# A transformer block on one core: block 0's divisions beside the projections, output projections ahead of the preceding block's last sums, and a tail that is written out

## The chip, the cores and the metric

The kernel runs on one core of a Trainium2 chip. A core has five engines with a queue of instructions each: TensorE (PE; its weight loads are listed apart as PEld), VectorE (DVE), ScalarE (ACT), GpSimd (POOL) and SyncE (SP), which issues nearly all DMAs here. The metric is device time in microseconds. The kernel before takes 1800.45 us, the median of 3 runs (1799.79 to 1802.5).

## The reference

One transformer block with adaptive layer norm, on 2048 rows of width 512, all in float32:

```python
mod = (_silu(c) @ w_mod).reshape(c.shape[0], 6, 1, -1)
sa, ca, ga, sb, cb, gb = (mod[:, i] for i in range(6))
h = _layernorm(x) * (1 + ca) + sa
x = x + ga * attention(h, wqkv, wo)          # 32 heads of 16, softmax over all 2048 keys
h = _layernorm(x) * (1 + cb) + sb
x = x + gb * (gelu_tanh(h @ w1 + b1) @ w2 + b2)   # 512 -> 1792 -> 512
```

The inputs are drawn large (the weights of the attention times 8, those of the feed-forward part times 64), so the softmax needs its row maxima.

## The kernel before, in words

**Precision.** Operands of TensorE are split into a high part (rounded to fp32r) and a low part (the remainder). A product is three matmuls: high by high, low by high, high by low. A "group" is the list of such terms that add into one bank of the matmul accumulator.

**Rows.** The 2048 rows are 4 blocks of 512 (`NB`, `TB`). A block's way after attention is: four *divisions* (`o_prep(b, k)`, one for each quarter of the 512 columns, that is for 8 heads); the output projection with residual (4 groups of 12 terms, one for each 128 rows); layer norm; 4 transposes with modulation; 14 pieces of the first feed-forward layer (`ffn1(i)`, 12 terms each) with the Gelu; and the sums of the second layer, in three parts (`PARTS`), 4 groups each. The last of these parts here is called the block's last sums.

**The attention loop.** There are 32 units: 4 blocks of queries by 8 sets of 4 heads. Each unit has 16 half steps of 128 keys, 512 in all (`half_step`). A half step issues 4 score matmuls (`e`, L623), whose exponent ScalarE takes (`p`, L628), 4 matmuls for the row maxima (`mx`, L382), whose maximum VectorE takes (`mxp`, L387), and the sums over values (`pv`, L652, 4 matmuls with 8 records). The maxima need a whole pass over the keys before the unit's first exponent, so they run `LEAD` = 84 matmuls ahead of the scores; a unit has 64. When a unit's 64 are done, VectorE and GpSimd make a high and a low part of the maxima, SP stores them to DRAM (`m<-m`, L408) and loads them back as two extra rows of the scaled queries (`qst<-m`, L414). The unit's first `e` waits for that load.

**Background work.** Beside the loop, one bank (number 7, named `bg`) takes the groups of projections and feed-forward work: six matmuls of half the rows each (`RUN` = 6) in a half step, the upper and lower 64 rows in turn. A generator hands out the groups in a written order (`work`): first `block0` (the query, key and value projections that are still missing, then `open_ffn`, which closes old buffers and opens new ones), then `ffn_block(0)`, `(1)`, `(2)`. It hands out nothing while its condition isn't met, and then the half step has no background work: the last score matmul of the step sits in bank 7 instead.

**The clock.** Work on other engines is put into the program by a count: `advance` adds 1 to it with each exponent, so 4 in a half step, and `later(n, f)` issues f after n counts. In the engines' queues everything then stands in the order in which it was issued. The division of `o_prep` is such a chain: SP loads the sums of exponents (`dn<-ou`, L682) and the sums over values (`ob`); 14 counts on VectorE inverts them (L692); SP stores them to DRAM (`rden`, L696) and loads them back spread over the heads' rows (`rb<-rden`, L700); then one engine multiplies and splits (L704 to L706): GpSimd, but VectorE for block 3. At most two divisions are under way, and none starts before `open_ffn` has run.

```python
        eng = gp if b < NB - 1 else ve
...
        later(14, inv)
...
        if not ready or "f" not in pools:
            return
```

**Weights.** `wload` (L738) issues on SP the loads of the split weights, in the order of a list (`stream`), into 8 buffers in turn, one in each second half step; a load waits on SP until the buffer's last matmul is done. Behind the loop 6 more buffers come.

**The Gelu.** In the loop it is taken apart: ScalarE takes a tanh, and GpSimd does seven instructions for each piece (L853 to L863). Only block 3, behind the loop, uses ScalarE's own Gelu (`evac_tail`).

**Behind the loop** (L1040 on, the tail) the matmuls have all 128 rows and 7 banks in turn. What is left of block 2 is handed out in turn with block 3's projection and norm: the generator of block 3 (`last`) is asked first, and where it has nothing, block 2's groups come. The last unit's sums still have to go through their division there.

Of the kernel before, what the change touches and what calls it, by code (L numbers as in the profile page):

```python
# [16 lines left out]
P = 128  # L17
S = 2048
D = 512
# [18 lines left out]
LEAD = 84  # L38
# [24 lines left out]
PARTS = ((0, 6), (6, 12), (12, NF))  # L63
AHEAD = 2
# [5 lines left out]
def block_kernel(ctx: ExitStack, tc: tile.TileContext, x, wqkv, wo, w1, b1, w2, b2, c, w_mod, out):  # L70
# [71 lines left out]

    hcm, hpool = pool("hT", side="right")
    hT = [[hpool.tile([P, KC, TB], FR, name=f"hThi{b}"), None] for b in range(NB)]
# [24 lines left out]
    def load_x(b, q=sy):  # L169

        xin[b] = hpool.tile([P, 4, D], F32, tag=f"lo{b}", name=f"xin{b}", bufs=1)
# [296 lines left out]
    def low_x(b, f, e):  # L468
        if hT[b][1] is None:
            hT[b][1] = hpool.tile([P, KC, TB], FR, tag=f"lo{b}", name=f"hTlo{b}", bufs=1)  # L470
# [97 lines left out]
    first[0] = False  # L568
    vgcm, vgpool = pool("vg", bufs=2)
# [67 lines left out]
    def attn_out(u, pv):  # L637
# [3 lines left out]
        later(2, lambda: sy.dma_start(ou_d[qb][g], o))  # L641
        if g % 2:
            later(8, lambda: ready.append((qb, g // 2)))
# [19 lines left out]
    x2_t = []  # L663

    def open_ffn():
# [4 lines left out]
        pools["pc"] = [f.tile([P, 2, TB], FR, name=f"pc{i}") for i in range(KC)]  # L670
        pools["x2"] = [f.tile([P, D], F32, name=f"x2{i}") for i in range(4)]

    def tmp(name):
        return pools["f"].tile([P, D], F32, tag="t", name=name, bufs=8)

    free_pc, busy = [0], [0]

    def o_prep(b, k):
# [7 lines left out]
        tgt = pools["pc"][k] if b < NB - 1 else pc_t[k]  # L686
        eng = gp if b < NB - 1 else ve
# [15 lines left out]
        def div():  # L703
            eng.tensor_tensor(ob, ob, rb, op=ALU.mult)  # L704
            eng.tensor_copy(tgt[:, 0], ob)
            eng.tensor_tensor(tgt[:, 1], ob, tgt[:, 0].bitcast(F32), op=ALU.subtract)  # L706
# [5 lines left out]
    def try_prep():  # L712
        if not ready or "f" not in pools:
# [14 lines left out]
    stream, at = [], 0  # L728
    for b in range(NB):
        stream += [(b, "o", k) for k in range(KC)]  # L730
        at = 0
        for lo, hi in PARTS:
            top = min(hi + AHEAD, NF)
            stream += [(b, 1, i) for i in range(at, top)] + [(b, 2, i) for i in range(lo, hi)]
            at = top
    wt, used, ringed, extra = {}, set(), [], []
# [17 lines left out]
    def ffn_block(b):  # L754

        tail = b == NB - 1
        f = pools["f"]
        x2, pc = (x2_t, pc_t) if tail else (pools["x2"], pools["pc"])
        parts, at = [], 0
        for lo, hi in PARTS:  # L760
            top = min(hi + AHEAD, NF)
            parts.append((range(at, top), lo, hi))
            at = top
        gt = {}

        def w(*key):
            return wt[(b, *key)]

        def loaded(*keys):
            return until(lambda: all((b, *k) in wt for k in keys))  # L770

        def drop(*keys):
            used.update((b, *k) for k in keys)

        def load_x2():
            for t in range(4):
                r0 = b * TB + t * P
                sy.dma_start(x2[t], x[r0 : r0 + P, :])

        later(0 if tail else 9, load_x2)  # L780
        yield from until(lambda: done[b] == KC - 1)
        yield from wait(4)
        yield from loaded(*[("o", k) for k in range(KC)])
        mv = small.tile([P, 4, 2], F32, tag="mv", name="mv")
        rs = small.tile([P, 4], F32, tag="rs", name="rs")
        three = ((0, 0), (0, 1), (1, 0))
        for t in range(4):
            sl = slice(t * P, (t + 1) * P)
# [5 lines left out]
            yield [(pc[i][:, a, sl], w("o", i)[:, c]) for i in range(KC) for a, c in three], "bg", evac  # L794
        drop(*[("o", k) for k in range(KC)])
        yield from wait(2)
        ln_factor(mv, rs)
        yield from wait(7)
# [302 lines left out]
```

## Time and profile before

| | |
|---|---|
| time, median of 3 runs (range) | 1800.45 us (1799.79 to 1802.5) |
| the profiled execution's own time | 1804.94 us |
| its span | 1803.1 us, mean granted clock 0.982 |
| TensorE matmuls | 1737.2 us busy, 96% |
| VectorE | 1390.1 us, 77% |
| ScalarE | 1245.8 us, 69% |
| GpSimd | 679.1 us, 38% |
| maxima, L387 | 1272.3 us of VectorE, 683 ns each |
| exponents, L628 | 1057.0 us of ScalarE, 603 ns each |
| adds of b2 in the loop, L814 | 1289 ns each on GpSimd |

The profile is of one execution of the program. A row of a timeline has the start, the duration (both in us), the engine, the line, the operation, the tiles written and read, and in brackets what the instruction waited for. A row of groups has the busy time and the mean of one in ns, then the idle time ahead of it and what ended that. TensorE is busy 96% of the span, but that is an average over stages: the opening up to about 113 us, the loop up to 1638 us and the tail have different limits, so the prediction reads each stretch by itself.

### The profile page before, as it was taken

Reading aid. Unit: us, or ns where it says so; the run is one execution under the profiler, and the core shown is the slowest. Engines: PE = TensorE matmul, PEld = TensorE weight load, DVE = VectorE, ACT = ScalarE, POOL = GpSimd, SP = SyncE. Lnnn points to the kernel's source line nnn. Section 1 sums busy time; section 2 is a strip of 40 time slices with the busy share of each in tenths; the row PEclk is TensorE's granted clock in tenths of the full one; section 3 lists DMA queues with packets and bytes.
Section 4 is the critical chain, followed back from the end, with each engine's and each line's share of the span. In section 5 each row is a group of like instructions: output and inputs, shape, how many; then the busy total and the mean of one; then the engine's idle time right before and its main releaser. Section 6 shows DMA issues by size and latency. Waiting matters only on the chain.

```text
span 1803.1 us, 32261 instructions
## 1 busy us (share of the span) xinstructions
PE 1737.2 (96%) x12013; PEld 900.9 (50%) x12013; DVE 1390.1 (77%) x2309; ACT 1245.8 (69%) x2373; POOL 679.1 (38%) x685
## 2 busy tenths in 40 slices
PE   7999999999998999999999999999999999998889
PEld 5654444444443444545454444444444444445677
DVE  7988888888887988888888988888888988700232
ACT  3367777777776677777877778877878778673131
POOL 7333444432112047603641037612641037525720
PEclk8999999999999999999999999999999999999899
DMA  8746767665467323425545533524454434213444
GB/s 283 211 154 196 227 184 230 200 194 142 137 162 184 90 71 106 114 66 137 142 112 161 139 85 101 132 54 131 123 130 128 128 104 111 76 39 112 177 150 163
DMA packets 137128, 251.88 MB, mean 140 GB/s; under 512 B 25854, under 2 KB 45324, under 8 KB 136972
## 3 DMA queue, kind: packets, MB, share of 16 engines
q1 hardware_dynamic: 135712, 248.19, 48.1%
q8 instruction: 95, 1.56, 0.4%
q10 hardware_dynamic: 1260, 1.63, 0.3%
q14 instruction: 61, 0.50, 0.1%
HBM read 188.49 MB, written 61.28 MB: 139 GB/s over the span
## 4 chain that ended last, share of the span: by engine, by line
PE 84%; DVE 6%; DMA 4%; POOL 2%; ACT 2%; issue 1%; SPq 0%; DVEq 0%; ACTq 0%; POOLq 0%
PE bg L269 42%; PE pv L652 26%; PE e L623 10%; DVE mxp L387 4%; PE mx L382 3%; DMA wm<-in_w_mod_dram 1%; DMA kh<-qk 1%; ACT p L628 1%; DMA qst<-m 1%; PE pr L269 0%; DMA rden<-dn 0%; DMA m<-m 0%; ACT h L829 0%; POOL s L860 0%; DVE x L791 0%
## 5 line engine op out<-in xcount | busy, mean ns | idle before, releaser
L387 DVE TENSOR_REDUCE mxp<-mx 128x1 f32<-128x512 f32 x2048 | 1272.3, 683 | 204.6 <-PE mx L382 178.4
L628 ACT ACTIVATE p<-e 128x512 f32<-128x512 f32 x2011 | 1057.0, 603 | 327.8 <-PE e L623 293.5
L382 PE MATMUL mx<-kh,qst 48*128 48x512 f32 x2048 | 869.2, 441 | 10.1 <-DVE mxp L387 7.7
L623 PE MATMUL e<-qst,kh 50*128 50x512 f32 x2011 | 739.7, 417 | 14.6 <-DMA qst<-m 7.1
L652 PE MATMUL pv<-p,vg 128*32 128x512 f32 x4096 | 548.4, 607 | 0.0
L623 PEld LDWEIGHTS e<-qst,kh 50*128 50x128 f32 x2011 | 370.1, 187 | 165.6 <-ACT p L628 145.2
L382 PEld LDWEIGHTS mx<-kh,qst 48*128 48x128 f32 x2048 | 370.4, 186 | 42.7 <-DVE mxp L387 36.8
L269 PE MATMUL bg<-w,g 64*128 64x512 f32 (+1 forms) x1056 | 283.8, 407 | 14.2 <-DMA w<-w2s 8.2
L269 PEld LDWEIGHTS bg<-w,g 64*128 64x128 f32 (+1 forms) x1056 | 186.9, 187 | 158.9 <-ACT p L628 87.6
L269 PE MATMUL bg<-pc,w 64*128 64x512 f32 (+1 forms) x888 | 247.4, 411 | 0.0
L269 PEld LDWEIGHTS bg<-pc,w 64*128 64x128 f32 (+1 forms) x888 | 154.3, 186 | 143.8 <-ACT p L628 90.7
L269 PE MATMUL bg<-hThi,wqkv 64*128 64x512 f32 x560 | 169.1, 421 | 0.1
L269 PEld LDWEIGHTS bg<-hThi,wqkv 64*128 64x128 f32 x560 | 93.4, 186 | 119.0 <-ACT p L628 106.0
L652 PEld LDWEIGHTS pv<-p,vg 128*32 128x32 f32 x4096 | 80.8, 108 | 129.4 <-issue 123.2
L807 POOL TENSOR_TENSOR x<-y,x 128x512 f32<-128x512 f32 x36 | 46.2, 1290 | 216.3 <-ACT y L806 216.3
L860 POOL TENSOR_SCALAR s<-s 128x512 f32<-128x512 f32 x42 | 62.9, 1497 | 115.6 <-ACT s L858 111.5
L269 PE MATMUL bg<-wo,pc 64*128 64x512 f32 x288 | 81.5, 415 | 1.8 <-DVE x L791 1.2
L269 PE MATMUL bg<-hTlo,wqkv 64*128 64x512 f32 x280 | 76.4, 392 | 0.0
L269 PEld LDWEIGHTS bg<-wo,pc 64*128 64x128 f32 x288 | 50.3, 188 | 49.8 <-ACT p L628 26.8
L403 POOL CAST m<-mt 128x32 fp32r<-128x32 f32 x32 | 6.7, 210 | 166.5 <-DVE mt L401 166.5
L853 POOL TENSOR_TENSOR s<-h 128x512 f32<-128x512 f32 x42 | 43.7, 1041 | 54.7 <-ACT h L852 54.6
L269 PEld LDWEIGHTS bg<-hTlo,wqkv 64*128 64x128 f32 x280 | 51.6, 184 | 10.9
(145 smaller groups left out, 1192.7 us busy)
## 6 DMA issues: line engine op xcount, KB each, us to landing
kh<-qk SPq DMA_DIRECT2D x256, 192.0 KB
w<-w2s SPq DMA_DIRECT2D x54, 512.0 KB
w<-w1s SPq DMA_DIRECT2D x52, 512.0 KB
vg<-v SPq DMA_DIRECT2D x64, 332.0 KB
qk<-parts SPq DMA_DIRECT2D x32, 512.0 KB
qst<-qk SPq DMA_DIRECT2D x64, 192.0 KB
qk<-parts SPq DMA_DIRECT2D x32, 256.0 KB
ou<-osb SPq DMA_DIRECT2D x32, 256.0 KB
```

The source lines that it names most:

```text
L269: return te.matmul(ps, term[0][r], term[1][r], start=i == 0, stop=i == n - 1)
L382: te.matmul(ps, qst[u][r0 : r0 + KR, p, qc * P : (qc + 1) * P], kh(u, kr // 2)[r0 : r0 + KR, p, (kr % 2) * TB : (kr % 2 + 1) * TB], start= ...
L387: ins = ve.tensor_reduce(mxp[u][:, hc, kr : kr + 1], ps, axis=AX.X, op=ALU.max, negate=True)
L403: gp.tensor_copy(m2[:, 0], mt)
L623: te.matmul(ps, kh(u, kc // 8)[r0 : r0 + KX, p, (kc % 8) * P : (kc % 8 + 1) * P], qst[u][r0 : r0 + KX, p], start=True, stop=True)
L628: saw(ac.activation(t, ps, AF.Exp, scale=SCALE))
L652: te.matmul(cur["ps"][32 * j : 32 * (j + 1)], vg[u][:, kc, j * VW : j * VW + 32], pt.pop(4 * s + j), start=kc == 0, stop=kc == NKC - 1)
L807: later(4, lambda: gp.tensor_tensor(x2[t], y, x2[t], op=ALU.add))
L853: gp.tensor_tensor(s, h, h, op=ALU.mult)
L860: gp.tensor_scalar(s, s, 1.0, None, op0=ALU.add)
```

## The change

Five things change.

- `LEAD` goes from 84 to 88.
- **Block 0's divisions.** Their targets (`pchi`, `pclo`) take the place of block 0's input rows, which are free when its last projection is done (`open_pc`); a pool of their own (`div`) holds the buffers. So they no longer wait for `open_ffn`, but run beside the last projections of the other blocks. `open_ffn` in turn waits until no division is under way.
- **Fronts and feeds.** `ffn_block` is split into `front` (output projection, norm, transposes) and `feed` (the two layers). `work` hands out the projection of block b + 1 ahead of block b's last sums, for blocks 1 and 2. The parts of the second layer are 6, 4 and 4 pieces instead of 6, 6 and 2. In the front, ScalarE copies the projection out of bank 7 and GpSimd adds the residual; before, VectorE did both in one add (L791). The norms are on GpSimd (for block 0 in part).
- **Block 3's divisions** are on GpSimd while the loop runs and on VectorE behind it. `wload` is also tried in the other half steps while fewer than four weights are loaded ahead.
- **The tail** is written out. First come block 2's groups, whose remaining first-layer pieces use ScalarE's Gelu, until three are left (`KEEP`); then block 3's projection over three of the four quarters, into four banks, and the last quarter when its division is done; then the norm on VectorE; then the three kept groups, the transposes, and block 3's feed-forward part.

```diff
-LEAD = 84
+LEAD = 88
...
-PARTS = ((0, 6), (6, 12), (12, NF))
-AHEAD = 2
+PARTS = ((0, 6, 8), (6, 10, NF), (10, NF, NF))
...
-        later(2, lambda: sy.dma_start(ou_d[qb][g], o))
+        late = u < NU - 1
+        later(2 * late, lambda: sy.dma_start(ou_d[qb][g], o))
...
+    def open_pc():
+        pcs.extend(rows_tile(0, n, "pc" + n) for n in ("hi", "lo"))
...
-        eng = gp if b < NB - 1 else ve
+        eng = ve if over[0] else gp
...
-        if not ready or "f" not in pools:
+        if not ready or not pcs:
...
             def evac(ps, t=t):
-                ve.tensor_tensor(x2[t], ps, x2[t], op=ALU.add)
-                later(0 if t == 3 or tail else 8, lambda: ln_stat(mv, t, x2[t]))
+                y = tmp("y")
+                ac.activation(y, ps, AF.Copy)
+                def add():
+                    gp.tensor_tensor(x2[t], y, x2[t], op=ALU.add)
+                    later(4, lambda: ln_stat(mv, t, x2[t]))
+                later(2, add)
...
         def norm(t):
-            (gp if t in (0, 2) and not tail else ve).tensor_scalar(
+            (gp if b or t in (0, 2) else ve).tensor_scalar(
...
+            if not pcs and not any(0 in p[2] for p in plan[n:]):
+                open_pc()
...
-        yield from until(lambda: not preps and not owed[0] and not vrows)
+        yield from until(lambda: not preps and not owed[0] and not vrows and not busy[0])
         open_ffn()
...
         for b in range(NB - 1):
-            yield from ffn_block(b)
+            for j in fronts[b]:
+                if j != "ln":
+                    yield j
+            for j in feed(b, pools["x2"][b % 2]):
+                if j != "last":
+                    togo[0] -= b == NB - 2 and j is not None
+                    yield j
+                elif b < NB - 2:
+                    for i in fronts[b + 1]:
+                        if i == "ln":
+                            break
+                        yield i
...
-        if h:
+        if h or len(wt) < len(used) + KC:
             wload()
...
+    KEEP = 3
+    while togo[0] > KEEP:
+        do(next(jobs))
...
+    banks = [take("o") for t in range(4)]
+    n = 3 * KC
+    for t in range(4):
+        for i, term in enumerate(o_terms(last, t, range(KC - 1))):
+            mm(banks[t], term, i, n)
+        advance()
+        try_prep()
+    while done[last] < KC - 1:
+        do(None)
...
+        for i, term in enumerate(o_terms(last, t, [KC - 1])):
+            mm(banks[t], term, n - 3 + i, n)
+        ve.tensor_tensor(x2[t], banks[t], x2[t], op=ALU.add)
+        ln_stat(mv, t, x2[t])
...
+    for j in jobs:
+        do(j)
+    banks = [take("o") for fc in range(KC)]
```

Three places in the engines' orders show what moves. The first is SP around unit 10's maxima (`m_102`): `rden` and `rb` are block 0's divisions, `w` the weights, `kh`, `qst` and `vg` the operands of the units to come. Before:

```order
L751 DMA w_7733<-w1s_136 128x1024
L355 DMA kh_191<-qk_88 48x2x512 x2
L696 DMA rden_128<-dn 128x32
L751 DMA w_7803<-w1s_137 128x1024
L696 DMA rden_128<-dn 128x32
L700 DMA rb<-rden_128 128x1x512
L751 DMA w_7878<-w1s_138 128x1024
L578 DMA vg<-v 128x664
L700 DMA rb<-rden_128 128x1x512
L355 DMA kh_192<-qk_88 48x2x512 x2
L578 DMA vg<-v 128x664
L408 DMA m_102<-m_7871 4x32x32 x2
```

And after, on the same engine around the same store:

```order
L767 DMA w_7642<-w1s_136 128x1024
L767 DMA w_7720<-w1s_137 128x1024
L359 DMA qst<-qk_84 48x2x512 x2
L359 DMA kh_191<-qk_88 48x2x512 x2
L767 DMA w_7810<-w1s_138 128x1024
L359 DMA kh_191<-qk_88 48x2x512 x2
L767 DMA w_7890<-w1s_139 128x1024
L412 DMA m_102<-m_7932 4x32x32 x2
L583 DMA vg<-v 128x664
L359 DMA kh_192<-qk_88 48x2x512 x2
L583 DMA vg<-v 128x664
L418 DMA qst<-m_102 2x1024 x2
```

The two stores and two loads of the divisions are gone from ahead of the maxima's store, and the value loads stand behind it.

The second is the place of two of block 3's divisions (`ob`) near the end of the loop. Before, they stand on VectorE among the maxima (`mxp`):

```order
L387 TENSOR_REDUCE mxp<-mx 128x1 x11
L704 TENSOR_TENSOR ob<-ob,rb 128x512
L705 CAST kh_193<-ob 128x512
L706 TENSOR_TENSOR kh_193<-ob,kh_193 128x512
L387 TENSOR_REDUCE mxp<-mx 128x1 x2
L704 TENSOR_TENSOR ob<-ob,rb 128x512
L705 CAST kh_193<-ob 128x512
L706 TENSOR_TENSOR kh_193<-ob,kh_193 128x512
L387 TENSOR_REDUCE mxp<-mx 128x1 x13
```

After, they stand on GpSimd, between two units' maxima splits (`m`):

```order
L407 CAST m_21596<-mt 128x32
L408 TENSOR_TENSOR m_21596<-mt,m_21596 128x32
L888 TENSOR_TENSOR x_7449<-y,x_7449 128x512
L888 TENSOR_TENSOR x_7450<-y,x_7450 128x512
L718 TENSOR_TENSOR ob<-ob,rb 128x512
L719 CAST kh_193<-ob 128x512
L720 TENSOR_TENSOR kh_193<-ob,kh_193 128x512
L718 TENSOR_TENSOR ob<-ob,rb 128x512
L719 CAST kh_193<-ob 128x512
L720 TENSOR_TENSOR kh_193<-ob,kh_193 128x512
L407 CAST m_22260<-mt 128x32
L408 TENSOR_TENSOR m_22260<-mt,m_22260 128x32
```

The same six instructions changed their engine, and the next unit's split stands directly behind them.

The third is TensorE in the tail, from block 3's output projection (`wo` by `kh`, in which the divided sums lie) to the first piece of its first layer; `g` marks block 2's last sums. Before:

```order
L269 MATMUL bg<-wo,kh_193 128x512 x6
L269 MATMUL bg<-wo,kh_189 128x512 x6
L269 MATMUL bg<-w_22936,g 128x512 x3
L269 MATMUL bg<-w_22938,g 128x512 x3
L269 MATMUL bg<-w_22936,g 128x512 x3
L269 MATMUL bg<-w_22938,g 128x512 x3
L827 MATMUL bg<-ident,xn 128x128 x16
L269 MATMUL bg<-kh_193,w_23063 128x512 x4
```

After, on TensorE at the same work, the end of the partial projections first:

```order
L273 MATMUL o<-wt_22945,kh_193 128x512 x3
L273 MATMUL o<-wt_22944,kh_193 128x512 x3
L273 MATMUL o<-wt_22943,kh_189 128x512 x3
L273 MATMUL o<-wo,kh_189 128x512 x12
L273 MATMUL bg<-w_22897,g 128x512 x3
L273 MATMUL bg<-wt_22948,g 128x512 x3
L273 MATMUL bg<-wt_22947,g 128x512 x3
L273 MATMUL bg<-wt_22946,g 128x512 x3
```

The projection is cut into three quarters and a last one (`wo`, 12 matmuls), and behind it stand three groups of 12 instead of two of 6 before the transposes.

More of the change, by code (lines that the diff above doesn't have):

```diff
@@ L752, in wload, with loaded @@
         wt[key] = t
[L754 to L780, printed above, removed]
+    def loaded(b, *keys):
+        return until(lambda: all((b, *k) in wt for k in keys))
@@ L816, in ffn_block, with norms @@
-        for t in range(4):
-            if t < 3 or tail:
-                norm(t)
-            else:
-                later(3, lambda: norm(3))
-            later(28 + 12 * t, lambda t=t: add_b2(t))
-        yield from wait(8)
+        def norms():
+            xn.extend(tmp("xn") for t in range(4))
+            for t in range(4):
+                later(3 * (t == 3), lambda t=t: norm(t))
+                later(28 + 12 * t, lambda t=t: gp.tensor_tensor(x2[t], x2[t], b2_b, op=ALU.add))
+        later(13, norms)
@@ L888, in evac @@
                         r0 = b * TB + t * P
[L889 to L893 removed]
+                        later(2 if over[0] else 8, lambda: sy.dma_start(out[r0 : r0 + P, :], x2[t]))
+                yield [(gt[i][0][:, a, sl], wt[b, 2, i][:, c]) for i in range(lo, hi) for a, c in three], "bg", evac
+            drop(b, *[(2, i) for i in range(lo, hi)])
     def block0():
```

201 lines of the change are left out of this document (122 added, 79 removed).

## The prediction

> **What bounds the kernel now.** I read the whole-span windows first, then the step length of the attention loop from the matmul timeline, then the waits, then the end in order of time. Windows (columns: stretch, its length, busy time of each engine with its instructions, granted clock, DMA share, GB/s), with the span from the page:
>
> ```profile
> span 1803.1 us, 32261 instructions
> ...
> 205.00:490.00 285.00, 284.92 (x2148) 139.92 (x2144) 240.65 (x397) 223.91 (x438) 96.78 (x105) 1.00 0.63 183
> 542.00:562.00 20.00, 19.02 (x114) 7.56 (x113) 17.23 (x30) 15.00 (x29) 6.35 (x6) 1.00 0.70 186
> 1638.36:1699.06 60.70, 44.54 (x168) 33.59 (x169) 3.11 (x4) 11.88 (x19) 51.78 (x48) 0.83 0.48 171
> 1699.06:1725.13 26.07, 21.21 (x88) 15.88 (x86) 15.71 (x21) 6.08 (x8) 13.12 (x12) 0.93 0.59 199
> 1725.13:1803.13 78.00, 74.40 (x325) 60.94 (x325) 18.27 (x26) 18.50 (x28) 4.05 (x3) 0.99 0.44 148
> ```
>
> Most of the loop has TensorE busy without a gap. 542 to 562 is a stretch without background work. The last three rows are the tail, from the loop's last sum over values at 1638.36: in the first of them TensorE is busy 44.54 of 60.70 us at a clock of 0.83 while GpSimd is busy 51.78. So the loop is at its limit except in a few places, and the tail is where time lies open.
>
> The length of a half step is the distance between two groups of pv matmuls (timeline, TensorE; start, duration). The first two rows stand eight full half steps apart, the next two eight steps without background work:
>
> ```profile
> 1201.48 1.06 PE L652 MATMUL pv<-p,vg 128*32 128x512 f32 x8
> ...
> 1224.81 1.07 PE L652 MATMUL pv<-p,vg 128*32 128x512 f32 x8
> ...
> 538.02 1.06 PE L652 MATMUL pv<-p,vg 128*32 128x512 f32 x8
> ...
> 559.93 1.06 PE L652 MATMUL pv<-p,vg 128*32 128x512 f32 x8
> ```
>
> A full step takes 23.33 / 8 = 2.92 us, an empty one 21.91 / 8 = 2.74. Six background matmuls of half the rows therefore cost 0.18 us where a step has room for them. The loop also stalls at three unit starts and once in unit 30. One row of the waits, then the pv rows around each stall:
>
> ```profile
> PE e L623 <- DMA qst<-m: 7.1, 3, 3.9
> ```
>
> ```profile
> 578.23 1.07 PE L652 MATMUL pv<-p,vg 128*32 128x512 f32 x8
> ...
> 590.99 1.06 PE L652 MATMUL pv<-p,vg 128*32 128x512 f32 x8
> ...
> 679.06 1.06 PE L652 MATMUL pv<-p,vg 128*32 128x512 f32 x8
> ...
> 691.50 1.07 PE L652 MATMUL pv<-p,vg 128*32 128x512 f32 x8
> ...
> 1528.55 1.06 PE L652 MATMUL pv<-p,vg 128*32 128x512 f32 x8
> ...
> 1533.19 1.07 PE L652 MATMUL pv<-p,vg 128*32 128x512 f32 x8
> ```
>
> They are 2, 3 and 1 steps apart: 12.76 - 5.84 = 6.9 us lost at unit 10, 12.44 - 8.76 = 3.7 at unit 12, 4.64 - 2.92 = 1.7 at unit 30, in all 12.3, of which 7.1 is the bare wait for the row maxima to come back into qst.
>
> **The change, part by part.** The sum is made against the profiled execution's span of 1803.1.
>
> *LEAD 84 to 88.* Four more maxima before the loop, where VectorE sets the pace:
>
> ```profile
> 103.91 7.32 DVE L387 TENSOR_REDUCE mxp<-mx 128x1 f32<-128x512 f32 x12 [0.41 <-PE mx L382]
> ```
>
> 4 x 7.32 / 12 = +2.4 us; the low end is nothing, if VectorE catches up before anybody waits. In return every unit has one step, 2.92 us, more between its last maximum and its first exponent.
>
> *Block 0's divisions.* Their DMAs leave the stretch behind the projections. Why unit 10 was late stands on SP (timeline):
>
> ```profile
> 568.71 0.60 SPq L700 DMA_DIRECT2D rb<-rden  x1
> ...
> 572.52 1.65 SPq L408 DMA_DIRECT2D m<-m  x2
> ...
> 581.92 0.54 SPq L414 DMA_DIRECT2D qst<-m  x2
> ```
>
> The store of the maxima stood behind two rb loads that waited for the rden stores, and landed only before 581.92, in heavy traffic. In the new order no division stands ahead of that store, and the step of LEAD comes on top: -6.9. Units 12 and 30 lost 3.7 and 1.7 beginning with bare waits under 2.92, so LEAD alone covers them: -5.4. By the built order the e matmuls that sit in bank 7, one for each empty step, fall from 37 to 16, because block 0's output projection starts 13 steps earlier and later ones stand ahead of the last sums. 21 steps are filled: 21 x 0.18 = +3.7 in the loop (from nothing, to 21 x 3 x 0.229 = 14 if the six halves cost what three full matmuls do in the tail, below), and their work leaves the tail.
>
> *Block 3's divisions move from VectorE to GpSimd inside the loop.* On VectorE they held the maxima up, with two pv rows that span the damage:
>
> ```profile
> 1555.68 0.68 DVE L704 TENSOR_TENSOR ob<-ob,rb 128x512 f32<-128x512 f32 x1
> ...
> 1562.06 2.48 DVE L387 TENSOR_REDUCE mxp<-mx 128x1 f32<-128x512 f32 x4
> ```
>
> ```profile
> 1556.42 1.07 PE L652 MATMUL pv<-p,vg 128*32 128x512 f32 x8
> ...
> 1569.52 1.07 PE L652 MATMUL pv<-p,vg 128*32 128x512 f32 x8
> ```
>
> Two steps took 13.10 instead of 5.84: -7.3. GpSimd also takes the adds of the front's twelve sums and four more norms. That this costs VectorE's maxima nothing: with GpSimd idle and with it busy (POOL is the fifth engine of the windows), 34.90 / 56 = 0.62 and 38.19 / 62 = 0.62 us a maximum (second pair: the maxima alone).
>
> ```profile
> 585.00:630.00 45.00, 43.93 (x309) 21.32 (x306) 40.34 (x70) 30.99 (x60) 0.46 (x2) 0.95 0.37 90
> 1080.00:1125.00 45.00, 45.00 (x342) 22.38 (x340) 38.54 (x64) 36.37 (x71) 32.93 (x33) 1.00 0.42 113
> ```
>
> ```profile
> 585.00:630.00 45.00, 34.90 (x56) 0.95 0.37 90
> 1080.00:1125.00 45.00, 38.19 (x62) 1.00 0.42 113
> ```
>
> ScalarE's copy of the front's sums replaces a VectorE add that bank 7 waited for in the same way: nothing. Loop in all: 2.4 + 3.7 - 6.9 - 5.4 - 7.3 = -13.5.
>
> *The tail.* Before it took 1803.1 - 1638.4 = 164.8 us. One full matmul, from the chain of waits; then the two places where it stood still and the LayerNorm (timeline):
>
> ```profile
> 1725.13 74.41 PE bg L269 x325
> ```
>
> ```profile
> 1670.31 1.62 PE L269 MATMUL bg<-w,g 128*128 128x512 f32 x3 [7.37 <-DMA w<-w2s]
> ...
> 1710.26 2.91 PE L269 MATMUL bg<-w,g 128*128 128x512 f32 x12
> ...
> 1716.39 3.70 PE L827 MATMUL bg<-ident,xn 128*128 128x128 f32 x15 [1.01 <-DVE xn L810]
> ```
>
> 74.41 / 325 = 0.229 us. The first stretch holds 168 matmuls, 38.5 us of work in 60.7: 22.2 lost, because six pieces of the Gelu run through GpSimd's seven instructions there. The second holds 88, 20.2 in 26.1: 5.9 lost around the LayerNorm. From the last matmul at 1799.55 to the end are 3.6. In the new order 520 matmuls and transposes stand behind the loop, 60 fewer than 580. Only two first-layer pieces are left there and both go through ScalarE's Gelu, so the 22.2 go; the cover of the last attention quarter's division is seven groups of 12, 19.2 us, and 36 partial projections, 8.2 more. Behind them three kept groups (36 x 0.229 = 8.2 us) hide the LayerNorm up to the transposes. What they can't hide is the modulation behind the transposes: from 1716.39 + 3.70 = 1720.09 to 1725.13, less 11 matmuls of 0.229, 2.5 us. New tail: 520 x 0.229 + 2.5 + 3.6 = 125.2, that is -39.6. If the Gelu's cover fails, 22.2 come back.
>
> One price there is open, the norms beside GpSimd's adds of b2, which now stand right behind them (groups by line and shape, the tail's and the loop's):
>
> ```profile
> L810 DVE TENSOR_SCALAR xn<-x2t,mv,rs 128x512 f32<-128x512 f32 x4 | 3.8, 1008 | 1.2 <-POOL rs L235 1.2
> ...
> L810 DVE TENSOR_SCALAR xn<-x,mv,rs 128x512 f32<-128x512 f32 x6 | 3.4, 562 | 0.0
> ...
> L814 POOL TENSOR_TENSOR x<-x,b_b 128x512 f32<-128x512 f32 x12 | 15.5, 1289 | 0.0
> ```
>
> Four norms took 3.8 us beside GpSimd, 1.008 each against 0.562. I take 3.8, which the kept groups cover. The Trainium skill (SBUF — State Buffer, Who interferes with whom) has a tensor_scalar of VectorE in its two-port mode and a GpSimd instruction share one pair of ports, the later one waiting out the whole of the other. By that rule the four norms would alternate with three adds of 1.289 us (L814) and take some 3 us longer, and the sum would be about 3 us higher; the trace's 1.008 agrees with part of such blocking.
>
> *Sum.* -13.5 - 39.6 = -53.1: a span of 1750.0. The profiled execution's own time was 1804.94, 4.5 above the runs' median of 1800.45; against that median I forecast 1800.45 - 53.1 = 1747.
>
> **The rivals.** *The maxima are late again.* wload is now tried in every half step while few weights are ahead, and a load on SP waits for its buffer's last matmul, ahead of a maxima store. For it: the stalls above came from that queue. Against: one step more of slack than any of them had at units 12 and 30. The 12.3 stay: 1747 + 12.3 = 1759.
>
> *The projection weights come late.* The three loads for the last output projection stand on SP behind rb. Rows of the same chain before:
>
> ```profile
> 1647.14 0.61 SPq L682 DMA_DIRECT2D dn<-ou  x1
> ...
> 1665.93 3.13 SPq L751 DMA_DIRECT2D w<-w2s  x6
> ```
>
> ```profile
> 1649.18 0.35 DVE L692 RECIPROCAL dn<-dn 128x32 f32<-128x32 f32 x1 [49.84 <-DMA dn<-ou]
> ```
>
> A small transfer took 2.0 us there, and weights issued at 1665.93 were used at 1670.31, 4.4 later. Three transfers, the copy of the sum and the reciprocal make some 7 us to rb, 11.5 to the first weight: ready before 19.2. At the 9.4 us that the maxima took from 572.52 to 581.92 it is 29 + 4.4, a wait of 14.5: 1762. I take the first, since only weights compete there.
>
> *Slower than before: GpSimd's queue.* A division waits for rb at the head of GpSimd's queue, and the next unit's maxima split stands behind it. The longest such wait before, from the waits (time, count, longest):
>
> ```profile
> POOL ob L704 <- DMA rb<-rden: 44.2, 8, 25.1
> ```
>
> It fell in a stretch where nothing needed GpSimd. From a unit's last maximum to its first e there were 84 - 64 = 20 maxima, five steps, and are now six, 17.5 us; two transfers at 2.0 and the split leave about 12 (an estimate). A hold of 25 then costs 13 us a unit; the gain of 53 is gone at the fourth such hold among 15 divisions, and five make it slower, 1747 + 5 x 13 = 1812. Against: with twelve divisions on GpSimd the run before lost 12.3 in all.
>
> *The filled steps don't fill.* 14 instead of 3.7: 1757.
>
> **How the numbers follow.** As summed 0.58 (1740 to 1755: LEAD, filled steps and modulation at nothing, or 8 above for the norms and half a stall); maxima late again 0.18; weights late 0.13; steps don't fill 0.05; GpSimd's queue 0.06. The range is 1738 to 1771, which holds the first four and the first two rivals nearly together. A measurement of this kernel tells 0.2%, 3.6 us, from no change; only the GpSimd case, and holds just short of it, come out there: faster 0.93, same 0.01, slower 0.06.
>
> **What would show it.** Right: the last pv row near 1625, no bare wait of e for qst<-m over 1 us, no VectorE multiply of ob before it; about 125 us from there to the end, with no wait of bg on GpSimd's g over 1 us. A loop that ends at 1637 speaks for the first rival; a wait of the tail's o matmuls on wt<-wos over 2 us for the second; GpSimd's ob waiting over 12 us for rb with a late m behind it for the third. The prediction is wrong if the loop lengthens, or if the tail keeps more than 135 us.

## The result and the profile after

The changed kernel takes 1746.91 us (median of 4 runs, 1745.46 to 1749.71) against 1800.12 before: a ratio of 0.9706, 95% interval 0.9688 to 0.9725, some 53 us. The forecast was 1747. Its profiled execution took 1745.46, with a span of 1743.7, 59.4 below the span of before and not 53. The forecast of the span was 1750.0, so the sum missed by 6 against the spans, while the medians agree. Where its parts were right and wrong is below.

The loop's stretch and the tail, from the windows of the kernel after (stretch, length, busy time of PE, PEld, DVE, ACT and POOL with instructions, clock, DMA share, GB/s):

```profile
span 1743.7 us, 32429 instructions
...
205.00:490.00 285.00, 284.90 (x2148) 139.42 (x2148) 241.04 (x400) 223.65 (x436) 106.82 (x115) 1.00 0.64 191
1616.31:1637.05 20.74, 19.31 (x85) 15.62 (x85) 3.92 (x7) 4.93 (x7) 7.20 (x8) 1.00 0.69 214
1637.05:1657.64 20.59, 20.01 (x85) 15.67 (x85) 12.51 (x25) 0.00 (x0) 4.78 (x6) 1.00 0.33 119
1657.64:1664.00 6.36, 3.38 (x22) 2.60 (x21) 5.61 (x8) 2.78 (x4) 6.20 (x7) 1.00 0.65 193
1664.00:1743.68 79.68, 76.03 (x332) 61.92 (x331) 19.65 (x27) 18.49 (x28) 1.11 (x1) 1.00 0.50 180
```

The steady stretch is what it was. In the tail TensorE is busy 118.7 of 127.4 us, at full clock, where the first stretch of the tail before had 0.83. The start and the end of the loop, from the timelines of after on TensorE and SP:

```profile
97.13 0.56 SPq L418 DMA_DIRECT2D qst<-m  x2
...
106.42 0.62 PE L628 MATMUL e<-qst,kh 50*128 50x512 f32 x1
...
112.72 1.93 PE L658 MATMUL pv<-p,vg 128*32 128x512 f32 x8
...
1613.78 2.53 PE L658 MATMUL pv<-p,vg 128*32 128x512 f32 x16
```

The last sum ends at 1613.78 + 2.53 = 1616.31, 22.0 us sooner than before, and the tail takes 127.4 us, 37.4 less. Between the first and the last sum no half step is longer than 3.8 us; before, two were near 9. A half step is measured here, and in what follows, from the end of one group of pv matmuls to the end of the next. The long waits for qst<-m and the VectorE multiplies in the loop are gone. What is left in the tail, from the waits and the timeline:

```profile
PE o L273 <- DMA wt<-wos: 2.0, 3, 1.4
```

```profile
1624.80 0.33 SPq L710 DMA_DIRECT2D rden<-dn  x1
...
1631.62 0.59 SPq L714 DMA_DIRECT2D rb<-rden  x1
1632.27 1.40 SPq L767 DMA_DIRECT2D wt<-wos  x3
...
1636.09 0.69 DVE L718 TENSOR_TENSOR ob<-ob,rb 128x512 f32<-128x512 f32 x1 [7.87 <-DMA rb<-rden]
...
1637.05 0.97 PE L273 MATMUL o<-wt,kh 128*128 128x512 f32 x3 [1.43 <-DMA wt<-wos]
...
1661.29 1.21 PE L273 MATMUL bg<-kh,w 128*128 128x512 f32 x4 [1.75 <-POOL kh L1144]
...
1663.74 21.70 PE L273 MATMUL bg<-kh,w 128*128 128x512 f32 x92 [1.24 <-POOL kh L1144]
```

520 matmuls of 0.229 are 119.1; the projection weights cost 2.0, the modulation 1.75 + 1.24, and the output some 3.6 behind the last matmul: 127.7 in all; the tail measured 127.4.

### The profile page after: what moved, and what is told of

Read it like the earlier page. It is cut to its first block, busy times and chain, and to the rows that moved or that the text cites. A ratio compares the mean times of both kernels' runs of the same rounds, so it can differ in the third digit from the quotient of the medians.

```text
span 1743.7 us, 32429 instructions
## 1 busy us (share of the span) xinstructions
PE 1710.1 (98%) x12061; PEld 884.7 (51%) x12061; DVE 1377.2 (79%) x2297; ACT 1241.0 (71%) x2377; POOL 686.4 (39%) x691
## 4 chain that ended last, share of the span: by engine, by line
PE 91%; DVE 4%; ACT 2%; DMA 1%; POOL 1%; issue 1%; SPq 0%; ACTq 0%; DVEq 0%; POOLq 0%
PE bg L273 45%; PE pv L658 29%; PE e L628 11%; PE mx L386 3%; DVE mxp L391 2%; PE pr L273 1%; ACT p L633 1%; DMA wm<-in_w_mod_dram 1%; PE o L273 1%; DVE hTlo L475 1%; ACT h L834 0%; PE mx L332 0%; DMA rden<-dn 0%; PE bg L832 0%; DMA wt<-wos 0%
## 5 line engine op out<-in xcount | busy, mean ns | idle before, releaser
L628 PE MATMUL e<-qst,kh 50*128 50x512 f32 x2032 | 753.8, 418 | 6.4 <-ACT p L633 6.2
L386 PEld LDWEIGHTS mx<-kh,qst 48*128 48x128 f32 x2048 | 370.0, 185 | 24.1 <-DVE mxp L391 18.8
L273 PE MATMUL bg<-w,g 64*128 64x512 f32 (+1 forms) x1044 | 277.8, 404 | 0.0
L273 PE MATMUL bg<-pchi,w 64*128 64x512 f32 (+1 forms) x656 | 194.5, 416 | 1.4 <-ACT p L633 1.4
L273 PEld LDWEIGHTS bg<-pchi,w 64*128 64x128 f32 (+1 forms) x656 | 109.0, 184 | 149.2 <-ACT p L633 101.4
L273 PE MATMUL bg<-pclo,w 64*128 64x512 f32 (+1 forms) x328 | 88.6, 389 | 0.0
L857 DVE TENSOR_TENSOR g<-h,g 128x512 fp32r<-128x512 f32 x16 | 11.1, 692 | 94.9 <-PE bg L273 63.8
L273 PEld LDWEIGHTS bg<-pclo,w 64*128 64x128 f32 (+1 forms) x328 | 60.5, 184 | 12.1
L273 PE MATMUL bg<-wo,pchi 64*128 64x512 f32 x192 | 64.8, 417 | 0.0
```

Of the source, the lines that this page charges most:

```text
L273: return te.matmul(ps, term[0][r], term[1][r], start=i == 0, stop=i == n - 1)
L386: te.matmul(ps, qst[u][r0 : r0 + KR, p, qc * P : (qc + 1) * P], kh(u, kr // 2)[r0 : r0 + KR, p, (kr % 2) * TB : (kr % 2 + 1) * TB], start= ...
L628: te.matmul(ps, kh(u, kc // 8)[r0 : r0 + KX, p, (kc % 8) * P : (kc % 8 + 1) * P], qst[u][r0 : r0 + KX, p], start=True, stop=True)
L857: ve.tensor_tensor(g[:, 1], h, g[:, 0].bitcast(F32), op=ALU.subtract)
```

## The experiments

A ratio is to the kernel before as it ran beside the experiment on the same chip, since that kernel's own median moved from one occasion to another (1800.12 to 1804.4).

**LEAD back to 84 in the changed kernel.**

```diff
-LEAD = 88
+LEAD = 84
```

> The changed kernel with LEAD back at 84. The theory: the move of block 0's divisions takes away unit 10's stall, LEAD those of units 12 and 30. In the changed kernel the maxima's store still waits some 5 us on SP in units 12, 13, 15, 16, 29 and 30 (a weight load whose buffer is not free yet stands ahead), and with one step of 2.92 less these loads land about when they are needed: bare waits of e for qst<-m in two to six units, 1 to 5 us in all, 1748 to 1752. The rival: LEAD carries nothing and only the move counts: no such wait, 1746 to 1747.

Measured: 1742.61 (1742.14 to 1743.12), ratio 0.9673 [0.9658, 0.9689]: faster than the changed kernel by 4 to 6 us (medians, ratios). The theory fails. The rival has the mechanism, since no `e` waits for qst<-m, but not the price: LEAD 88 carries nothing here and costs the start. The start, and the store of unit 12's maxima, in this kernel's timeline, with a window of its start:

```profile
97.43 0.57 SPq L418 DMA_DIRECT2D qst<-m  x2
...
103.65 0.50 PE L628 MATMUL e<-qst,kh 50*128 50x512 f32 x1
...
109.03 1.06 PE L658 MATMUL pv<-p,vg 128*32 128x512 f32 x8
...
660.61 1.17 SPq L412 DMA_DIRECT2D m<-m  x2
```

```profile
109.00:115.00 6.00, 6.00 (x49) 3.02 (x52) 5.38 (x10) 5.07 (x10) 1.08 (x1) 1.00 0.50 141
```

The same in the changed kernel, TensorE ahead of its first `e` and the window:

```profile
105.82 0.79 PE L386 MATMUL mx<-kh,qst 48*128 48x512 f32 x1 [1.05 <-DVE mxp L391]
```

```profile
109.00:115.00 6.00, 5.74 (x25) 2.76 (x26) 3.72 (x6) 3.15 (x6) 0.00 (x0) 0.50 0.37 110
```

From issue of the load to the first `e` are 6.22 us, against 9.29 at 88, where the four more maxima stand ahead of it and TensorE waits 1.05 us for VectorE. From there to the first pv are 5.38 against 6.30, and at 88 the granted clock is 0.50 behind that wait. It is 0.50 to 0.55 from 109 to 115 us in all seven profiled executions with LEAD 88; of the six with 84, five have 1.00 and the kernel before has 0.75. The six begin their pv between 109.0 and 112.1, the seven between 112.7 and 115.4: on the mean 3.6 later, where I had taken 2.4 for the maxima and nothing for the clock.

And the store, which I thought fixed at 5 us late in six units, is not: at 84 it follows VectorE's last step by 0.4 us in unit 12. Nor did a weight load hold it at 88. SP waits there for GpSimd, whose split of the maxima stands behind the second half of a Gelu piece (VectorE, GpSimd and SP at unit 12 of the changed kernel):

```profile
660.06 0.21 DVE L405 STREAM_TRANSPOSE mt<-mn 128x32 f32<-128x32 f32 x1
...
660.22 1.50 POOL L869 TENSOR_SCALAR s<-s 128x512 f32<-128x512 f32 x1 [3.63 <-ACT s L867]
...
665.07 0.22 POOL L407 CAST m<-mt 128x32 fp32r<-128x32 f32 x1
...
665.31 1.15 SPq L412 DMA_DIRECT2D m<-m  x2
```

With one step more of lead the maxima are ready at 660.27, 0.05 behind the start of four instructions of that piece. Units 13 and 30 show the same. No `e` waits for it, so this delay costs nothing here.

**LEAD 80 in the changed kernel.** (`LEAD = 80` in the same line.)

> The changed kernel with LEAD 80, one step less again. From 88 to 84 took 3.7 us off the start and cost no stall. The theory: at 80 a unit has four steps, 11.7 us, from its last maximum to its first exponent; the chain took 3.0 us to the load in most units and the load some 5.5 more, so the start gains 3.7 again and most units lose nothing: 1739 to 1741. The rival: store and load stand in the phase of the weight loads again (5.0 us as in six units at 88), 13.7 against 11.7, and two to six units lose 2 and more, each of which also lowers the granted clock: 1745 to 1760.

Measured: 1757.43 (1754.56 to 1759.44), ratio 0.9749 [0.9727, 0.9771]. The rival's sign and size, in another place: its waits are in the stretch of the projections, at units 5 and 6, not behind weight loads. At unit 6 the load of the maxima stands on SP behind a load of values (vg) that waits 5.5 us for the store of the values (v). From the waits, and from the timeline at unit 6 (SP, then TensorE):

```profile
PE e L628 <- DMA qst<-m: 3.8, 2, 2.5
```

```profile
391.88 1.83 SPq L412 DMA_DIRECT2D m<-m  x2
393.81 0.93 SPq L342 DMA_DIRECT2D v<-vst  x1
400.32 0.34 SPq L583 DMA_DIRECT2D vg<-v  x1
400.76 0.56 SPq L418 DMA_DIRECT2D qst<-m  x2
...
403.71 0.79 PE L628 MATMUL e<-qst,kh 50*128 50x512 f32 x1 [2.49 <-DMA qst<-m]
```

The start doesn't gain, it loses: the load is issued at 100.28, 2.85 later than at 84, the first `e` follows 6.22 us behind it as at 84, and the first pv begins at 113.65, 4.6 later than at 84, with the clock at 0.54 from 109 to 115. Why the load comes later isn't shown. Of the 17.3 us between the two profiled spans the loop's steps have 11.6, and the start has most of the rest.

**LEAD 88 alone, in the kernel before.**

```diff
-LEAD = 84
+LEAD = 88
```

> The kernel before with LEAD 88 alone. The theory: units 12 and 30 lose nothing (3.7 + 1.7), unit 10 loses 2.9 less, the start costs about 0.6: 1800 - 7.7 = 1792, and unit 10 keeps a stall of about 4. The rival: the stores slip by as much as the maxima come earlier, because they wait on SP for something that comes at a fixed time (the rden stores, a weight buffer): 1797 to 1801.

Measured: 1799.66, ratio 0.997 [0.996, 0.9981]: 5 us faster, not 8. The stalls of the units 10, 12 and 30 are all gone, which is more than the theory said, and the rival is out. But ahead of unit 10, among the empty steps, a new one stands. From the timeline of VectorE and TensorE, then the windows:

```profile
565.53 0.35 DVE L692 RECIPROCAL dn<-dn 128x32 f32<-128x32 f32 x1 [2.78 <-DMA dn<-ou]
...
566.49 0.50 PE L382 MATMUL mx<-kh,qst 48*128 48x512 f32 x1 [1.75 <-DVE mxp L387]
```

```profile
563.00:567.00 4.00, 2.25 (x12) 0.64 (x11) 1.47 (x4) 1.69 (x4) 0.00 (x0) 1.00 0.92 216
567.00:572.00 5.00, 5.00 (x18) 1.78 (x19) 3.41 (x8) 1.79 (x3) 0.46 (x2) 0.56 0.78 178
572.00:580.00 8.00, 8.00 (x34) 2.99 (x32) 4.97 (x8) 4.13 (x8) 3.16 (x3) 0.50 0.69 210
```

VectorE waits 2.78 us for a division's dn, with the maxima behind it; TensorE waits 1.75 for that. Then the granted clock falls to 0.56 and 0.50, and three steps take 7.17, 4.19 and 4.20 us instead of 2.78. All five profiled executions with late divisions have such a wait for dn in the loop, 1.4 to 2.8 us long; with the early ones it is 0.4 at most. So block 0's divisions do harm by two ways, SP's queue and VectorE's, and LEAD alone covers only the first.

**Block 0's divisions late again, in the changed kernel.**

```diff
-        if not ready or not pcs:
+        if not ready or "f" not in pools:
```

> The changed kernel with block 0's divisions held until open_ffn has run, as before; LEAD stays 88. By the built order 28 steps are empty instead of 16 and 36 more full matmuls stand behind the loop: 36 x 0.229 = +8.2, less 12 filled steps at 0.14 to 0.18, -2. Unit 10 loses 6.9 - 2.9 = 4 again if the divisions were what made its maxima late: 1757. The rival, that LEAD alone covers unit 10: 1753 and no wait for qst<-m.

Measured: 1771.75 (1770.31 to 1773.33), ratio 0.9835 [0.9818, 0.9852]: this one condition is worth 23 to 25 us, more than twice what I expected. Unit 10's store was 6.9 us late again and no `e` waited for it, so that point goes to the rival. The two steps with the dn wait took 6.57 and 4.19 (of 2.78). The main part is the tail: 149.7 us instead of 127.4, where 36 matmuls are only 8.2. From its timeline:

```profile
1640.05 12.87 PE L273 MATMUL bg<-wt,g 128*128 128x512 f32 x45 [5.37 <-DMA wt<-w2s]
...
1660.24 4.21 PE L273 MATMUL o<-wo,kh 128*128 128x512 f32 x9 [3.86 <-DMA wo<-wos]
```

The new tail loads no weights between its first three and the issue of the last division. With more of block 2 left over, that lands on TensorE, and the granted clock is 0.83 to 0.86 from 1640 to 1690. Earlier weight loads were not tried in this kernel, but in the next.

**The projections behind the last sums, in the changed kernel.**

```diff
-            if hi == NF and b < NB - 2:
-                stream += [(b + 1, "o", k) for k in range(KC)]
...
-        if b == NB - 2:
+        if b < NB - 1:
...
-                elif b < NB - 2:
-                    for i in fronts[b + 1]:
...
```

> The changed kernel with each block's output projection behind the preceding block's last sums, as before. By the built order 26 steps are empty instead of 16 and 30 more full matmuls stand behind the loop: 30 x 0.229 = +6.9, less 10 steps at 0.14 to 0.18, -1.6: 1752. The rival, that a filled step costs what its matmuls take in the tail (0.69): no difference, 1747.

Measured: 1761.25 (1759.9 to 1763.11), ratio 0.9777 [0.9761, 0.9794]: 13 to 14 us slower than the changed kernel, not 5. The tail is 18.8 longer, with waits of 5.2 for w2s and 3.4 for wos. To see whether these are the excess, the next kernel adds

```diff
-        if done[last] < KC - 1:
-            try_prep()
-        else:
-            wload()
+        try_prep()
+        wload()
```

> The changed kernel with the projections behind the last sums (as in a_front_after, 1761.25) and with weight loads tried at every group behind the loop, not only when block 3's divisions are done. The theory: of the 18.8 us that this tail was longer, 6.9 are the 30 matmuls more, and the rest is the wait for weights (5.2 for w2s, 3.4 for wos) with the lower clock behind it: 1761 - 10 = 1751. The rival: the weights compete with the division's transfers and the wait only changes its name: 1757 to 1762.

Measured: 1753.57 (1750.96 to 1754.62), ratio 0.9727 [0.9706, 0.9748]. The waits are gone and the tail is 137.5, 8.7 us shorter. The theory holds within 3 us: the order of the projections is worth about what I took, 4 us by the ratios and 7 by the medians, and the rest of the 14 was the held weight loads. In the new order they show as the 2.0 us of waits for the projection weights. The changed kernel with this second edit alone, the exact counterpart, was not run.

**Block 3's divisions: on VectorE in the changed kernel, and on GpSimd in the kernel before.**

```diff
-        eng = ve if over[0] else gp
+        eng = ve if b == NB - 1 else gp
```

> The changed kernel with all of block 3's divisions on VectorE. The theory: VectorE stands still for rb among the maxima, and the loop loses about the 7.3 of before: 1754, with two long half steps near unit 29 or 30 and an ob multiply on VectorE ahead of them. The rival: the step more of LEAD gives the maxima room, and nothing or less than 3 is lost: 1747 to 1750.

Measured: 1749.86 (1748.74 to 1750.7), ratio 0.9712 [0.9696, 0.9728]. That is 1 to 3 us above the changed kernel, and the intervals overlap. Two steps take 4.0 us instead of 2.92: 2.2 us in the loop, the rival's case. VectorE doesn't wait for rb there; the three instructions are simply in the way (0.57 and 0.29 us of wait on TensorE). The other way round:

```diff
-        eng = gp if b < NB - 1 else ve
+        eng = gp if not x2_t else ve
```

> The kernel before with block 3's divisions on GpSimd as long as the loop runs, the last one on VectorE. The theory: the stall at unit 30 goes, 7.3 us: 1793. The rival: GpSimd then waits for rb in the same place, unit 31's maxima split stands behind it, and the stall of 7.3 comes back as a wait of e for qst<-m: 1796 to 1801.

Measured: 1805.08 (1799.47 to 1822.3) against 1804.4 beside it, ratio 1.001 [0.9989, 1.0032]: nothing. The rival's result, by a way I hadn't named. GpSimd's timeline and window in this kernel, then ScalarE and TensorE:

```profile
1557.46 1.29 POOL L704 TENSOR_TENSOR ob<-ob,rb 128x512 f32<-128x512 f32 x1
...
1549.00:1570.00 21.00, 17.86 (x115) 8.86 (x113) 10.37 (x18) 13.30 (x26) 18.87 (x19) 0.86 0.12 45
```

```profile
1563.87 0.63 ACT L858 ACTIVATE s<-s 128x512 f32<-128x512 f32 x1 [3.61 <-POOL s L855]
...
1565.04 0.79 PE L623 MATMUL e<-qst,kh 50*128 50x512 f32 x1 [3.13 <-ACT p L628]
...
1565.76 1.93 PE L652 MATMUL pv<-p,vg 128*32 128x512 f32 x8
...
1570.90 1.94 PE L652 MATMUL pv<-p,vg 128*32 128x512 f32 x8
```

GpSimd doesn't wait for rb. It is busy 18.87 of 21 us with Gelu pieces and the two divisions among them. The next piece is late by that, ScalarE stands 3.61 us at its tanh (L858) with the exponents behind it in its queue, and TensorE waits 3.13 us for an exponent; its steps there take 7.39 and 5.15. The split of unit 31's maxima also comes late, at 1569.42, but no `e` of that unit waits for it.

In the changed kernel the same divisions meet a free GpSimd, because block 2 has come to its second layer by then:

```profile
1537.97 1.28 POOL L718 TENSOR_TENSOR ob<-ob,rb 128x512 f32<-128x512 f32 x1 [3.42 <-DMA rb<-rden]
...
1532.00:1553.00 21.00, 21.00 (x156) 10.16 (x152) 17.57 (x32) 16.27 (x33) 8.62 (x10) 1.00 0.08 28
```

So neither the engine nor the place alone took the 7.3 us away: in the new place VectorE loses 2 and GpSimd nothing; in the old place both lose about the whole.

**ScalarE's Gelu behind the loop, in the kernel before.**

```diff
-                          ... "bg", evac_tail if tail else evac
+                          ... "bg", evac_tail if tail or x2_t else evac
```

> The kernel before with ScalarE's Gelu for those of block 2's first-layer pieces that stand behind the loop. The theory: GpSimd's chain is the whole of the 22.2 us that TensorE stood still from 1638 to 1699: 1778. The rival: part of it is the wait for weights (7.4 us were put down to w<-w2s) and the last division (rb was issued 27 us behind the loop's end): 1785 to 1790.

Measured: 1788.48 (1786.74 to 1790.03) against 1804.4, ratio 0.9913 [0.9899, 0.9927]. Its tail is 151.5 instead of 164.8: 13.3 of the 22.2 us. The rest is what the rival said in part, waits for weights with the clock at 0.91 over the first 40 us, and the wait of 0.74 for osb, which no Gelu touches:

```profile
1636.33 3.32 PE L269 MATMUL bg<-w,g 64*128 64x512 f32 x12 [0.74 <-ACT osb L640]
...
1663.19 4.77 PE L269 MATMUL bg<-w,g 128*128 128x512 f32 x12 [2.93 <-DMA w<-w2s]
```

**No kept groups, in the changed kernel.** (`KEEP = 0`.)

> The changed kernel with KEEP 0: the three kept groups stand ahead of block 3's projection. The theory: the norm is open now, TensorE stands still from the end of the projection to the first transposes; in the changed kernel the norm's last instruction ends 8.9 us behind the projection's last matmul, of which the kept groups fill 8.2. The wait of 2.0 for the projection weights goes in return, being covered by 8.2 more of work: +8.2 - 2.0 less what the transposes overlap, about +5.5, 1752. The rival: the kept groups only fill what the division's wait would have taken: 1747.

Measured: 1757.38 (1756.73 to 1759.69), ratio 0.9743 [0.9726, 0.9759], 0.37 percentage points or 6.7 us above the changed kernel (10.5 by the medians). The norm is open:

```profile
1667.05 3.04 PE L1139 MATMUL o<-ident,xn 128*128 128x128 f32 x12 [5.52 <-DVE xn L1132]
```

The theory holds for the wait: the kept groups hide 5.5 us of norm. The time is 5 us above what I expected, and the granted clock of 0.72 to 0.82 between 1660 and 1690 was not in the sum.

**A better version.** LEAD 84, and the projection weights ahead of the division's store and load:

```diff
     load_x2(last, x2)
+    for _ in range(3):
+        wload()
```

> The changed kernel with LEAD 84 and, behind the loop, three more weight loads right behind block 3's input rows, so that the three projection weights are issued ahead of the division's store and load. The theory: the last quarter's division isn't what TensorE waits for, the projection weights are, because they were issued only behind rb: the waits of 1.4 + 0.3 + 0.3 us go, 1742.6 - 2.0 = 1740.6. The rival: the loads slow the division's own small transfers, which then end the wait: 1742 to 1746, with the wait on the last quarter (kh) in place of wt<-wos.

Measured: 1740.77 (1739.91 to 1742.46), ratio 0.966 [0.964, 0.968], the fastest kernel of this study by its median; its interval overlaps that of LEAD 84 alone. No matmul of the projection waits any more, and the tail is 125.6. A last one then keeps four groups and puts one behind the transposes:

```diff
-    KEEP = 3
+    KEEP = 4
...
-    for j in jobs:
-        do(j)
+    while togo[0] > 1:
+        do(next(jobs))
     banks = [take("o") for fc in range(KC)]
...
+    for j in jobs:
+        do(j)
     ring("bg", (4, 5, 7, 6, 0, 1, 2, 3))
```

> As a_l84_wo_early (1740.77), with four groups kept (KEEP 4) and the last of them put behind the transposes, where in the changed kernel TensorE waited 1.75 and 1.24 us for the modulation (kh). The theory: the group's 2.75 us fill these waits, and the division needs no more than the six groups ahead of it now: 1740.8 - 2.8 = 1738. The rival: the division or the projection weights end the wait now that their cover is one group shorter (16.5 us behind the loop): 1740 to 1743, with a wait on wt<-wos or on the last quarter.

Measured: 1746.51 (1743.29 to 1747.24), ratio 0.9686 [0.9671, 0.9701]: worse. The waits for the modulation are gone, and another takes their place (VectorE, then TensorE):

```profile
1659.79 0.68 DVE L884 TENSOR_TENSOR x<-bg,x 128x512 f32<-128x512 f32 x1
...
1660.57 1.67 PE L273 MATMUL bg<-kh,w 128*128 128x512 f32 x4 [4.08 <-issue]
```

The matmul starts 0.10 us behind the end of that add. The add empties the bank of the group that I moved, and stands on VectorE behind the modulation; the ring of banks begins anew at bank 4 there. That the two share that bank follows from the code and fits the times; a kernel with another bank was not tried.

## Why the prediction was right, and where it was not

**The total** agrees with the medians to 0.1 us, and that is luck. The sum was made against one execution that took 1804.94, 4.5 above the median. Against the two profiled spans, which it was made from, it is too small: measured 59.4, sum 53.1, with the loop 8.5 short and the tail 2.2 too good. How much of that execution's excess stood in the terms isn't shown.

**The tail, -39.6 forecast, -37.4 measured: right in mechanism and size.** ScalarE's Gelu and the kept groups each showed in an experiment of their own (13.3 us in the kernel before, 6.7 to 10.5 in the changed one); the fewer matmuls show by their count alone (520 for 580, at 0.229 each). The term "If the Gelu's cover fails, 22.2 come back" gave the Gelu too much: with it alone 9 of the 22.2 stayed, beside waits for weights, a low clock and small waits, and went only with the rest of the new tail. Mis-sized by 2.0 was the term of no wait for the projection weights: the step "Three transfers, the copy of the sum and the reciprocal make some 7 us to rb" measured 15.3 (1616.31 to 1631.62). The store of rden alone took 6.8 to the next issue. The rival on late weights was thus half true; its price was 2.0 and not 14.5 (its own figures give 29 + 4.4 - 19.2 = 14.2), since the first weight came 20.7 us behind the loop, just past its cover of 19.2. The modulation cost 3.0 against 2.5.

**The norms** beside GpSimd's adds took 3.9 us for four, as forecast, but the row of before was misread: its mean of 1.008 mixes two kinds of norm, and so does the 1.045 of after. Two norms end before the first add begins, two meet an add (groups of VectorE up to 1655.2 and from 1655.6, then the third norm and the first add):

```profile
L1132 DVE TENSOR_SCALAR xn<-x2t,mv,rs 128x512 f32<-128x512 f32 x2 | 1.0, 541 | 0.0
...
L1132 DVE TENSOR_SCALAR xn<-x2t,mv,rs 128x512 f32<-128x512 f32 x2 | 3.0, 1549 | 0.0
```

```profile
1655.31 1.58 DVE L1132 TENSOR_SCALAR xn<-x2t,mv,rs 128x512 f32<-128x512 f32 x1
1655.31 1.29 POOL L1137 TENSOR_TENSOR x2t<-x2t,b_b 128x512 f32<-128x512 f32 x1
```

The third norm ends 0.29 us behind the end of the first add, the fourth 0.28 behind the second: each takes 1.0 us more than one by itself, 2.0 in all. By the rule on the shared ports in the Trainium skill (SBUF — State Buffer, Who interferes with whom) the later of a two-port tensor_scalar and a GpSimd instruction waits out the whole of the other. These two norms agree with it. The 3 us more in the prediction (4 x 0.562 + 3 x 1.289 - 3.8 gives 2.3) didn't come because two norms met an add here, as two had met a GpSimd instruction before (1.48 each, the others 0.53), so the 3.8 already held that price.

**The loop, -13.5 forecast, -22.0 measured: right in sign, wrong in three terms.** Step by step the 22.0 are: +1.5 at the start, -6.9 at unit 10, -3.7 at unit 12, -1.7 at unit 30, -7.3 at block 3's divisions, -3.8 in the last step, -1.2 and -1.8 in two lone steps at units 9 and 19, and the rest, +2.8, is about what the filled steps cost. Three terms were wrong. First, "LEAD alone covers them: -5.4". LEAD did cover the stalls of units 12 and 30 when it was alone in the old order, but in the new order nothing was left to cover: with 84 there is no stall either. LEAD 88 is a price of 4 us without return, and the term on the start, +2.4, was too small: 3.6 on the mean of all executions, with the lowered clock that it left out (in this pair +1.5, as the kernel before began late). Second, the divisions of block 0: I saw only SP's queue. They also held VectorE up at the change to block 0's feed-forward part, with waits for dn of 1.4 to 2.8 us and, where they were long, a lowered clock behind them; the early divisions removed both. In the profiled execution of before this was 1.2 us, in the one with LEAD 88 alone 7.2. Third, the sum had no term for the loop's last step, 5.3 us before, because 18 matmuls of half rows stood alone in it, and 1.5 after: -3.8.

**Block 3's divisions, -7.3: the amount is right, the reason was not.** That GpSimd takes the divisions and VectorE's maxima are free would have given nothing in the old place. In the new place VectorE itself would have lost 2.2 of the 7.3, so the order is worth some 5 and the engine some 2: block 2's work has advanced, and no Gelu stands on GpSimd there. LEAD isn't it: with 88 alone in the kernel before, the two steps take 9.10 and 4.13 us, as long as ever. Why VectorE loses less in the new place isn't shown.

**The filled steps:** bank 7 holds a score matmul in 16 steps instead of 37, as built, and the filled ones became ordinary full steps of 2.92 against a mean of 2.78 for the empty ones: 21 x 0.14 = +2.9. The rival of 14 is out.

**GpSimd's queue as the rival on the slower side** didn't appear in the changed kernel: the longest wait of a division for rb was 7.9 us, where 25.1 stood before (waits of after):

```profile
POOL ob L718 <- DMA rb<-rden: 14.7, 7, 7.9
```

The second half of its mechanism is there: the split of the maxima stood 5 us behind a Gelu piece in six units, and the slack covered it. And GpSimd's queue did take back the whole gain in the kernel before with the divisions moved, but by ScalarE's tanh and the exponents behind it, which the rival didn't name.

## What to carry to other kernels

A step that is moved should be costed with what else stands on the target engine at that place; the same move to another engine gave nothing in the old order and 1 to 3 us in the new one. An engine with time to spare can still hold the pace by whoever waits for it in order: a late GpSimd stopped TensorE by a tanh on ScalarE. A lead is worth its price only while something waits without it, so after each change of order try it smaller: here it had become pure cost, until one step less again cost some 14. And take a profiled execution's own excess out of the terms before they are added, or the sum and the median agree by accident.

## What the runs showed of the hardware

A wait of TensorE under 2 us can cost far more than itself. In the run with LEAD 88 alone, 1.75 us of waiting, in 4 us in which TensorE was busy for 2.25, was followed by 13 us at a granted clock of 0.50 to 0.56, and three steps lost 7.2 us. The Trainium skill (TensorE: Matmul & The Clock Gate, Part 1: The HAM clock gate (the "warmup" mystery)) has the half clock come after an idle window of some 3.4 us; here no wait was that long, only a thin stretch. The start with LEAD 88 shows the same: TensorE waits 1.05 us and is busy 4.75 of 6 us, and the next 6 us have a clock of 0.50; with LEAD 84 it is busy 5.16 of 6, and the clock stays at 1.00 in five of six executions. In full background work, waits of 0.57 and 0.29 us (the changed kernel with the divisions on VectorE) left the clock alone. And a transfer of 16 KB through DRAM, store and load back, isn't a fixed price: with weights and input rows in flight behind the loop, the store of rden took 6.8 us to the next issue where I had taken some 2.
